# Two temporaries for a scan's output weights, idle matmuls in the start-up, and another rule for late fills, in a planned attention-and-scan kernel

## The chip, the cores and the metric

The kernel runs on one core of a Trainium2 chip. The metric is the device time of one execution in microseconds (us); the figure given for a kernel is the median of its runs. A profile is of one further execution.

## What is computed

Two independent things are computed and laid side by side. The left 640 columns of the output are a diagonal complex scan: `h[t] = Lam_bar * h[t-1] + B_bar x[t]` over 2048 steps with 640 states, then `y = 2 Re(C h) + x * Dskip`. The right 640 columns are attention with 32 query heads of width 20 that share one key and one value head.

```python
Lam_bar = exp(dt * Lam);  B_bar = ((Lam_bar - 1) / Lam)[:, None] * Bmat
h = Lam_bar * h + Bu[:, t, :]            # 2048 steps, complex, 640 states
y = 2.0 * einsum("blp,dp->bld", hseq, Cmat).real + x * Dskip

q = (x @ wq).reshape(B, S, 32, 20);  k = x @ wk;  v = x @ wv
p = softmax(einsum("bhqd,bkd->bhqk", q, k) * 20 ** -0.5)
out_b = einsum("bhqk,bkd->bhqd", p, v).reshape(B, S, 640) @ wo
```

In the kernel the factor `(Lam_bar - 1) / Lam` is not put into `B` but into `C`: the scan's output weights `CGre` and `CGim` are the complex product of `C` with that factor and 2. They are the weights of the first half of the title.

## The kernel before, in words

**Units of attention.** The scores are made in units of 128 keys by 512 queries of one head. 32 groups (8 for each block of 512 queries) hold 4 heads and 16 key chunks each, so 64 units: 2048 in all. A unit's exponential goes one of two ways. By ScalarE: a tile of 2 or 3 units is filled by TensorE in PSUM (`fill_op`, L1245; tiles `R0` of 3 banks and `R1` of 2), and one activation turns it into weights (`ex_op`, L1260; recorded at L1263). By VectorE ("D unit"): TensorE writes the scores into one of the banks `B0`, `B1` or the lent third bank of `R0`, one instruction turns them into the bits of a 16-bit float (`dx_op`, L1269), and three more shift copies of them (`sh_op`, L1274, up to three units in one instruction). The four copies are averaged by TensorE, which needs four PV matmuls for such a unit where the ScalarE way needs one. `want_d` (L1230) decides on each fill whether a D unit goes with it: when a bank is free and VectorE's backlog is small.

**The scan.** It runs in 20 units (4 blocks of 512 steps by 5 chunks of 128 states), through three threads. `scan_in` (L889): ten matmuls and two VectorE products (L901) of `B x` by rotations. `scan_unit` (L907): GpSimd adds in pieces of 128 columns (`uh`, 8 pieces), VectorE scans (L928, two instructions), GpSimd rotates back (`tm4` to `tm7`, 16 pieces) and combines into `W` (8 pieces); all GpSimd pieces are recorded at L917. `y_tile` (L943): the matmuls of `W` with `CGre` and `CGim`, with the output copy at L962. `W` of the next block is only written when the four y tiles of the block before are made. How far the scan may run ahead is set by `scan_open` (L1160), which spreads its 20 units over the first 0.6 or 0.7 of the attention units.

**The output weights.** For each of 5 chunks and each of `CGre`, `CGim`, GpSimd multiplies one raw half by a column of `sc` in five pieces of 128 columns (L858) into the one float32 temporary `ctmp`, which lies in `tm4` to `tm6`, and VectorE does the rest with one instruction over 640 columns (L860). The raw halves come by ten transposing DMAs on SyncE's queue (SP), into the memory of `W` (and `ostage` for the last chunk). In the thread `sc` all this stands behind the scan's constants, two memsets and the eight loads of `WO4`. `prog["c"]` turns 1 with the last of them, and the first rotation back waits for it.

**What sets the order.** Nothing is scheduled by hand. `Plan` (L21) keeps a clock for each engine and adds instructions one by one; `main` (L1127) collects the next instruction of every thread, of the fills, exponentials, shifts and PV matmuls, gives each a key (the planned begin, a bias by kind, a little noise) and takes the smallest. Engines' queues are then in exactly this order. The lengths are the planner's own: a GpSimd piece of 128 columns is planned at `max(0.2, 128/450 + 0.1)`, 0.38 us. A matmul other than a fill may go ahead of the next fill only if it ends before that fill's begin plus `after[n % 2]` (L1339), 0.1 to 0.2 us for even tiles and 0.35 to 0.5 us for odd ones. `vary` (L1113) draws biases and limits like these anew in each of 64 turns, from the list `SEEDS`. Where the planner sees TensorE wait long at low load it puts in matmuls by zero (`PV<-cs,VP`, L1418). At the start-up, `setup` ends with the thread `rest` (two VectorE copies of a half of K, the V matmuls, six more); until it is done no PV matmul is planned, while fills and exponentials already run.

Of the kernel before, what the change touches and what calls it, by code (L numbers as in the profile page):

```python
# [9 lines left out]
ALU = mybir.AluOpType  # L10
AX = mybir.AxisListType
FP32 = mybir.dt.float32
# [231 lines left out]
class _Kernel:  # L244
    S, D, H, DH = 2048, 640, 32, 20
    NC, NQB, NKC, NGG = 5, 4, 16, 8
# [8 lines left out]
    SPARE = 0.33  # L255
# [9 lines left out]
    SEEDS = (19006, 20002, 21006, 22006, 23001, 24003, 25001, 26002, 27008, 28003, 0, 30006, 31008, 32005, 33006,  # L265
# [28 lines left out]
    def alloc(self):  # L294
# [67 lines left out]
        self.ctmp = self.tm[:].rearrange("p i n -> p (i n)").bitcast(FP32)[:, 1024:1664]  # L362
# [454 lines left out]
    def scan_ops(self):  # L817
# [4 lines left out]
        sa, su, sr, sy, sc_ = [], [], [], [], []  # L822
        self.prog = prog = dict(x=0, a=0, u=0, s=0, r=0, y=0, w=0, c=0)
# [9 lines left out]
        ct = [f"tm{i}{h}" for i in (4, 5, 6) for h in self.PIECES]  # L833
# [14 lines left out]
        for c in range(NC):  # L848
            for i, nm in ((0, "cre"), (1, "cim")):
                sc_.append(self.dma(K.Craw[c][:, i, :], t[nm][:, 128 * c:128 * (c + 1)], f"craw{c}{i}",  # L850
                                    writes=[f"Craw{c}{i}"] + ([f"ostage{i}"] if c == 4 else []), tr=True, kb=160))
        for c in range(NC):
            cr, ci = K.Craw[c][:, 0, :], K.Craw[c][:, 1, :]
            keys = [f"Craw{c}0", f"Craw{c}1", "sc"] + (["ostage0", "ostage1"] if c == 4 else ws)
            for (dst, x, y, gx, gy, op, nm) in ((K.CGre, cr, ci, GRE, GIM, ALU.subtract, "CGre"),
                                                (K.CGim, ci, cr, NGRE, NGIM, ALU.add, "CGim")):
                for i in range(0, 640, 128):
                    pool(lambda e, y=y, c=c, gy=gy, i=i: e.tensor_scalar(K.ctmp[:, i:i + 128], y[:, i:i + 128], sc[:, gy, c:c + 1],  # L858
                                                                         None, op0=ALU.mult), keys, [f"ct{i}"] + ct * (i == 0), 128)
                dve(lambda e, dst=dst, x=x, op=op, c=c, gx=gx: e.scalar_tensor_tensor(  # L860
                    out=dst[:, c, :], in0=x, scalar=sc[:, gx, c:c + 1], in1=K.ctmp, op0=ALU.mult, op1=op),
                    keys + ct + [f"ct{i}" for i in range(0, 640, 128)], [nm], 695)
        sc_[-1].done = lambda: prog.update(c=1)
# [16 lines left out]
        sx = [o for b in (1, 2, 3) for o in self.load_xa(b, lambda b=b: prog["y"] >= 4 * (b - 1), lambda b=b: prog.update(x=b))]  # L880
        return sc_, sy, sr, su, sa, sx
# [25 lines left out]
    def scan_unit(self, dve, pool, back, b, c):  # L907
# [68 lines left out]
    def dense_ops(self, qb):  # L976
# [5 lines left out]
        have = lambda: all(g in self.normed for g in range(self.NGG * qb, self.NGG * qb + (6 if qb == self.NQB - 1 else 8))) and (  # L982
# [130 lines left out]
    def vary(self, seed):  # L1113
# [11 lines left out]
        self.open, self.first = r.choice((0.6, 0.7)), r.choice(("sy", "proj", None))  # L1125

    def main(self):  # L1127
# [24 lines left out]
        sc_, sy, sr, su, sa, sx = (deque(x) for x in self.scan_ops())  # L1152
# [16 lines left out]
        threads = [("rest", rest), ("norm", norm), ("dense", dense), ("proj", proj), ("qt", qt), ("qr", qr), ("sy", sy), ("sa", sa), ("su", su), ("sr", sr), ("sc", sc_), ("sx", sx), *fins]  # L1169
# [142 lines left out]
        while True:  # L1312
# [14 lines left out]
            if cur["fill"] < cur["act"] + 2 and any(x < 64 for x in taken) and not early:  # L1327
                n = cur["fill"]
                g = next(i for i in range(NG) if taken[i] < 64)
                if g in qt_done:  # L1330
# [8 lines left out]
                    t_fill = (t_fill, t_fill + self.after[n % 2])  # L1339
# [191 lines left out]
```

## Time and profile before

| | us |
|---|---|
| time, median of 3 runs (lowest, highest) | 770.16 (769.84, 772.17) |
| the profiled execution's own time | 770.28 |
| its span, first to last instruction | 768.6 |
| ScalarE busy, of it in the exponentials (L1263, 677 instructions) | 752.5, 733.1 |
| VectorE busy | 708.3 |
| TensorE busy | 704.8 |
| GpSimd busy, of it in the output weights (L858, 50 instructions) | 446.0, 41.8 |
| mean granted TensorE clock (1 is full) | 0.989 |

The profiled execution takes 1.7 us more than its span, and 0.1 us more than the median of the runs. In the group lines the columns are: line, engine, operation, output and input, count; then busy time in all and the mean of one in ns; then the idle time of the engine just before them and what ended it. In lines of stretches each engine's busy time stands with its instructions in brackets, then the clock granted to TensorE, the share of the DMA engines and GB/s. Exponentials overlap at their ends, so their mean of one is longer than their step.

### The profile page before, as it was taken

The numbers are of one execution on the slowest core, as the hardware profiler recorded it, in microseconds if no ns is written. First come the engines' busy times: TensorE is split into PE (matmuls) and PEld (weight loads), VectorE is DVE, ScalarE is ACT, GpSimd is POOL, SyncE is SP. The second block draws the span as 40 slices with busy tenths as digits, with TensorE's granted clock in tenths as the row PEclk, the third lists the DMA queues.
The fourth block names the chain that finished last, engine by engine and source line by source line (L and its number), as shares of the span: only waits on it lengthen the run. The fifth ranks groups of instructions, "written<-read, shape, count | busy, mean of one in ns | idle before, by whom it ended". The sixth has DMA issues, their size and how long they took to land.

```text
span 768.6 us, 16664 instructions
## 1 busy us (share of the span) xinstructions
PE 704.8 (92%) x6538; PEld 213.4 (28%) x6538; DVE 708.3 (92%) x1236; ACT 752.5 (98%) x710; POOL 446.0 (58%) x867
## 2 busy tenths in 40 slices
PE   5799988888889999998889999988889999889998
PEld 2222222222222333322223323322223332223333
DVE  5599999999998999999997999999999789999986
ACT  8999999999999999999999999999999999999995
POOL 5612354579989931088997300199986469990040
PEclk9899999899999999999999999999999999999999
DMA  9366301000021100220002100040000201000020
GB/s 186 57 143 134 74 16 49 8 24 14 3 51 30 42 8 27 56 60 15 15 9 67 42 23 9 23 93 10 15 15 28 66 33 34 14 15 17 18 61 35
DMA packets 61179, 31.50 MB, mean 41 GB/s; under 512 B 41510, under 2 KB 61102, under 8 KB 61102
## 3 DMA queue, kind: packets, MB, share of 16 engines
q1 hardware_dynamic: 59606, 30.14, 15.9%
q8 instruction: 52, 0.85, 0.5%
q10 hardware_dynamic: 1496, 0.30, 0.2%
q14 instruction: 25, 0.20, 0.1%
HBM read 9.21 MB, written 12.69 MB: 28 GB/s over the span
## 4 chain that ended last, share of the span: by engine, by line
ACT 74%; PE 15%; DVE 9%; POOL 1%; DMA 1%; issue 1%; ACTq 0%; DVEq 0%; POOLq 0%
ACT P L1263 72%; PE R L421 5%; PE PV L421 5%; PE B L421 4%; DVE Pd L1274 4%; DVE Pd L1269 3%; DVE hh L928 1%; DVE tm L901 1%; POOL tm L858 1%; DMA WO<-in_B_wk_dram 1%; ACT cs L691 1%; ACT Pd L690 0%; ACT KT L538 0%; DVE CGre L860 0%; ACT L503 0%
## 5 line engine op out<-in xcount | busy, mean ns | idle before, releaser
L1263 ACT ACTIVATE P<-R 128x1024 bf16<-128x1024 f32 (+1 forms) x677 | 733.1, 1354 | 4.3 <-PE R L421 1.8
L421 PE MATMUL R<-QT,KT 32*128 32x512 bf16 (+1 forms) x1685 | 266.9, 389 | 48.6 <-ACT P L1263 37.1
L1269 DVE TENSOR_SCALAR Pd<-B 128x512 int16<-128x512 f32 x363 | 245.5, 682 | 19.4 <-PE B L421 17.0
L1274 DVE TENSOR_SCALAR Pd<-Pd 128x1536 int16<-128x1536 int16 (+2 forms) x513 | 260.2, 541 | 0.4
L421 PE MATMUL PV<-Pd,VP 128*32 128x512 bf16 x1744 | 256.9, 386 | 2.0 <-DVE OTr L1307 1.0
L421 PE MATMUL PV<-P,VP 128*32 128x512 bf16 x1612 | 253.3, 389 | 0.7 <-DVE OTr L1307 0.6
L917 POOL TENSOR_TENSOR tm<-hh,cs 128x128 bf16<-128x128 f32 x320 | 163.9, 533 | 17.7 <-DVE hh L928 8.3
L421 PEld LDWEIGHTS R<-QT,KT 32*128 32x128 bf16 (+1 forms) x1685 | 66.1, 91 | 301.0 <-ACT P L1263 271.0
L421 PE MATMUL B<-QT,KT 32*128 32x512 bf16 x363 | 141.0, 389 | 0.0
L917 POOL TENSOR_TENSOR uh<-tm 128x128 bf16<-128x128 bf16 x160 | 81.0, 527 | 97.6 <-DVE tm L901 93.7
L917 POOL TENSOR_TENSOR W<-tm 128x128 bf16<-128x128 bf16 x160 | 93.5, 608 | 49.4 <-PE B L421 45.3
L421 PEld LDWEIGHTS PV<-Pd,VP 128*32 128x32 bf16 x1744 | 60.1, 94 | 65.7 <-issue 40.5
L421 PEld LDWEIGHTS PV<-P,VP 128*32 128x32 bf16 x1612 | 58.1, 94 | 58.8 <-issue 46.6
L1011 POOL TENSOR_TENSOR OTd<-OTd,rwide 128x128 bf16<-128x128 bf16 x80 | 33.2, 443 | 60.0 <-DMA OTd<-o_rows 58.2
L1269 DVE TENSOR_SCALAR Pd<-R 128x512 int16<-128x512 f32 x73 | 49.9, 683 | 3.0 <-PE R L421 2.4
L901 DVE TENSOR_TENSOR tm<-B,cs 128x1024 bf16<-128x1024 f32 x40 | 48.5, 1213 | 1.0 <-PE B L421 0.6
L858 POOL TENSOR_SCALAR tm<-W,sc 128x128 f32<-128x128 bf16 x40 | 32.3, 821 | 27.5 <-DVE CGre L860 15.9
L421 PE MATMUL B<-CGre,W 128*128 128x384 bf16 (+1 forms) x160 | 46.4, 305 | 0.0
L421 PE MATMUL B<-CGim,W 128*128 128x384 bf16 (+1 forms) x160 | 45.5, 299 | 0.0
L928 DVE TENSOR_TENSOR_SCAN hh<-sc,hini,uh 128x512 f32<-128x512 f32 x30 | 40.7, 1358 | 0.0
L421 PEld LDWEIGHTS B<-QT,KT 32*128 32x128 bf16 x363 | 32.9, 91 | 0.0
L421 PE MATMUL B<-xaT,BTre 128*128 128x512 bf16 x100 | 30.1, 384 | 0.1
(149 smaller groups left out, 437.2 us busy)
## 6 DMA issues: line engine op xcount, KB each, us to landing
o_rows<-OTr SPq DMA_DIRECT2D x32, 128.0 KB, 1.7
QT<-q_rows SPq DMA_DIRECT2D x30, 128.0 KB, 2.2
q_rows<-Qd SPq DMA_DIRECT2D x16, 160.0 KB, 2.9
OTd<-o_rows SPq DMA_DIRECT2D x16, 160.0 KB, 3.4
out_dram<-ystage SPq DMA_DIRECT2D x16, 160.0 KB, 1.9
out_dram<-ostage SPq DMA_DIRECT2D x12, 160.0 KB, 1.8
P<-in_B_wq_dram SPq DMA_DIRECT2D x1, 800.0 KB, 5.6
WO<-in_B_wo_dram SPq DMA_DIRECT2D x4, 200.0 KB, 3.4
```

The lines of the kernel that those rows point to most:

```text
L421: ins = e.matmul(o() if callable(o) else o, lhsT=l, rhs=r, start=st, stop=sp, skip_group_check=True, **kw)
L691: act(lambda e, c=c, b=b: e.activation(K.cs[:, c, :, :].rearrange("p i n -> p (i n)"), K.tri[:, 4 * b + 2:4 * b + 4, :].rearrange("p r n - ...
L858: pool(lambda e, y=y, c=c, gy=gy, i=i: e.tensor_scalar(K.ctmp[:, i:i + 128], y[:, i:i + 128], sc[:, gy, c:c + 1], None, op0=ALU.mult), key ...
L901: dve(lambda e, k=k, h=h: e.tensor_tensor(K.tm[:, 2 * k:2 * k + 2, :], bass.AP(tensor=K.BB, offset=512 * int(h.key[1]), ap=[[512 * self.BA ...
L917: put(lambda e, c0=c0, end=end: e.tensor_tensor(out[:, c0:end], a[:, c0:end], b[:, c0:end], op), reads, [writes + h], n, gate=None if i el ...
L928: dve(lambda e, ri=ri, ini=ini: e.tensor_tensor_scan(K.hh[:, ri, :], dec, K.uh[:, ri, :], ini, ALU.mult, ALU.add), ["sc", *(f"uh{ri}{h}" f ...
L1011: ops.append(Op("pool", lambda e, c=c, m=m: e.tensor_tensor(K.OTd[:, m, c], K.OTd[:, m, c], K.rwide[:, c], ALU.mult), rw + [f"OTe{dd}" for ...
L1263: return Op("act", lambda e: e.activation(dst, K.R[n % 2][:, 0:512 * size], ACT.Exp, scale=self.exp_scale), [f"R{n % 2}"] + ["R0c"] * (siz ...
L1269: return Op("dve", lambda e: e.tensor_scalar(K.Pd[:, 0, u, :], K.B[x][:, :], self.d_off, 0.0, op0=ALU.add, op1=ALU.max), [key], [f"Pd{u}_0 ...
L1274: return Op("dve", lambda e: e.tensor_scalar(K.Pd[:, i, a:b, :], K.Pd[:, 0, a:b, :], float(self.SHIFTS[i]), 0.0, op0=ALU.subtract, op1=ALU ...
```

## The change

Five edits and a new list of seeds.

1. **Output weights.** `ctmp` becomes two temporaries of 640 float32 columns in `OTd`, the attention's tile that is first written at the end of the first 8 groups. The thread `sc` is split in four: the raw loads (`sl`, now ahead of everything else of `sc`), the constants and `WO4` (`sc`), GpSimd's products (`sk`) and VectorE's halves (`sg`). The products may run one temporary ahead of VectorE.
2. **Planned length.** These 50 GpSimd pieces are planned at 0.58 us each.
3. **Gates.** The rotations back no longer wait for the weights; the writes of `W` do, and so do the first normalisation loads into `OTd` (`have`). The loads of `xa` for block 1 wait until VectorE has made three of the ten halves.
4. **Idle matmuls** (`WARM`). From the second copy of `rest` until the first PV matmul of group 0, where the planner sees TensorE wait over 0.25 us and its load in the last 3.4 us is under 0.8, it adds matmuls of the identity with `xbT` into `B0`.
5. **Late fills.** How late a fill may be goes by the size of the last tile that waits for ScalarE (3 units: 0.35 to 0.5 us; else 0.1 to 0.2 us), not by the parity of the tile's number. `open` may also be drawn as 0.8.

```diff
-    SPARE = 0.33
+    SPARE, WARM = 0.33, 0.8
-    SEEDS = (19006, 20002, 21006, 22006, 23001, 24003, 25001, 26002, 27008, 28003, 0, 30006, 31008, 32005, 33006,
+    SEEDS = (3005, 4007, 5003, 6007, 7004, 0, 9002, 10005, 11003, 12003, 13007, 14005, 0, 16003, 17005, 18006,
...
-        self.ctmp = self.tm[:].rearrange("p i n -> p (i n)").bitcast(FP32)[:, 1024:1664]
+        self.ctmp = self.OTd[:].rearrange("p c n -> p (c n)").bitcast(FP32).rearrange("p (i n) -> p i n", i=2)
...
+        for c in range(NC):
+            for i, nm in ((0, "cre"), (1, "cim")):
+                sl.append(self.dma(K.Craw[c][:, i, :], t[nm][:, 128 * c:128 * (c + 1)], f"craw{c}{i}",
+                                   writes=[f"Craw{c}{i}"] + ([f"ostage{i}"] if c == 4 else []), tr=True, kb=160,
+                                   done=(lambda c=c: prog.update(l=c + 1)) if i else None))
...
+        wide = lambda fn, reads, writes, n, **k: sk.append(Op("pool", fn, reads, writes, occ=0.58, **k))
...
+                for i in range(0, 640, 128):
+                    wide(lambda e, y=y, c=c, gy=gy, i=i, h=h: e.tensor_scalar(K.ctmp[:, h, i:i + 128], y[:, i:i + 128], sc[:, gy, c:c + 1],
+                                                                            None, op0=ALU.mult), keys, [f"ct{h}{i}"], 128,
+                         gate=lambda n=2 * c + h: prog["g"] >= n - 1 and prog["l"] > n // 2, done=(lambda n=2 * c + h + 1: prog.update(k=n)) if i == 512 else None)
+                cd(lambda e, dst=dst, x=x, op=op, c=c, gx=gx, h=h: e.scalar_tensor_tensor(
+                    out=dst[:, c, :], in0=x, scalar=sc[:, gx, c:c + 1], in1=K.ctmp[:, h, :], op0=ALU.mult, op1=op),
...
+                    gate=lambda n=2 * c + h: prog["k"] > n, done=lambda n=2 * c + h + 1: prog.update(g=n, c=int(n == 2 * NC)))
...
-        sx = [o for b in (1, 2, 3) for o in self.load_xa(b, lambda b=b: prog["y"] >= 4 * (b - 1), lambda b=b: prog.update(x=b))]
+        sx = [o for b in (1, 2, 3) for o in self.load_xa(b, lambda b=b: prog["y"] >= 4 * (b - 1) and prog["g"] > 2, lambda b=b: prog.update(x=b))]
...
-                   gate=lambda: prog["s"] > u and prog["c"], done=(lambda: prog.update(r=u + 1)) if i == 3 else None)
-        free = lambda: prog["y"] >= 4 * b
+                   gate=lambda: prog["s"] > u, done=(lambda: prog.update(r=u + 1)) if i == 3 else None)
+        free = lambda: prog["y"] >= 4 * b and prog["c"]
...
-        self.open, self.first = r.choice((0.6, 0.7)), r.choice(("sy", "proj", None))
+        self.open, self.first = r.choice((0.6, 0.7, 0.8)), r.choice(("sy", "proj", None))
...
+        self.still = False
+        rest[1].done = lambda: setattr(self, "still", True)
...
-                    t_fill = (t_fill, t_fill + self.after[n % 2])
+                    t_fill = (t_fill, t_fill + self.after[bool(tiles) and len(tiles[-1][1]) == 3])
...
+                if self.still and not any(begun[0]) and owner[0] in (None, "rest") and "B0" not in o.keys()[1]:
+                    while t - p.begin("pe", (), ("B0",)) > 0.25 and self.load(t) < self.WARM:
+                        self.go(self.mms([self.m1(K.B[0], K.ident[:, :], K.xbT[:, 0, 0:512], True, True)], ["ident", "xbT0"], ["B0"],
+                                         kind="zero"))
```

More of the change, by code (lines that the diff above doesn't have):

```diff
@@ L821, in scan_ops @@
         t = self.t
-        sa, su, sr, sy, sc_ = [], [], [], [], []
-        self.prog = prog = dict(x=0, a=0, u=0, s=0, r=0, y=0, w=0, c=0)
+        sa, su, sr, sy, sc_, sl = [], [], [], [], [], []
+        self.prog = prog = dict(x=0, a=0, u=0, s=0, r=0, y=0, w=0, c=0, k=0, g=0, l=0)
         def mk(ops, eng):
@@ L847, in scan_ops @@
                 sc_.append(self.dma(dst, src, f"wo{j}{w}", reads=["WO4"], writes=[f"WO4_{j}{w}"], kb=200 if w else 50))
[L848 to L863, printed above, removed]
         for b in range(4):
@@ L879, in scan_ops @@
                 self.y_tile(sy, mk(sy, "dve"), b, q)
-        sx = [o for b in (1, 2, 3) for o in self.load_xa(b, lambda b=b: prog["y"] >= 4 * (b - 1), lambda b=b: prog.update(x=b))]
-        return sc_, sy, sr, su, sa, sx
+        sx = [o for b in (1, 2, 3) for o in self.load_xa(b, lambda b=b: prog["y"] >= 4 * (b - 1) and prog["g"] > 2, lambda b=b: prog.update(x=b))]
+        return sl, sc_, sk, sg, sy, sr, su, sa, sx
     def load_xa(self, b, gate=None, done=None):
@@ L981, in dense_ops @@
         ops = []
-        have = lambda: all(g in self.normed for g in range(self.NGG * qb, self.NGG * qb + (6 if qb == self.NQB - 1 else 8))) and (
+        have = lambda: self.prog["c"] and all(g in self.normed for g in range(self.NGG * qb, self.NGG * qb + (6 if qb == self.NQB - 1 else 8))) and (
             qb == 0 or qb - 1 in self.projected)
@@ L1151, in main @@
         qr = deque(o for g in range(2, NG) for o in self.qr_ops(g, lambda g=g: qt_done.add(g)))
-        sc_, sy, sr, su, sa, sx = (deque(x) for x in self.scan_ops())
+        sl, sc_, sk, sg, sy, sr, su, sa, sx = (deque(x) for x in self.scan_ops())
         n_sa = len(sa)
```

12 lines of the change are left out of this document (10 added, 2 removed), and 8 rows, old and new, of the table SEEDS.

## The prediction

> **What bounds the kernel.** I read the engines' shares first, then the groups of instructions, the waits, and last the busy time by stretches, since a mean hides stages.
>
> ```profile
> PE 704.8 (92%) x6538; PEld 213.4 (28%) x6538; DVE 708.3 (92%) x1236; ACT 752.5 (98%) x710; POOL 446.0 (58%) x867
> ...
> L1263 ACT ACTIVATE P<-R 128x1024 bf16<-128x1024 f32 (+1 forms) x677 | 733.1, 1354 | 4.3 <-PE R L421 1.8
> ...
> L1269 DVE TENSOR_SCALAR Pd<-B 128x512 int16<-128x512 f32 x363 | 245.5, 682 | 19.4 <-PE B L421 17.0
> L1274 DVE TENSOR_SCALAR Pd<-Pd 128x1536 int16<-128x1536 int16 (+2 forms) x513 | 260.2, 541 | 0.4
> ...
> L1269 DVE TENSOR_SCALAR Pd<-R 128x512 int16<-128x512 f32 x73 | 49.9, 683 | 3.0 <-PE R L421 2.4
> ```
>
> ScalarE is the bound, but not a fixed one: it has what VectorE doesn't take. VectorE made 363 + 73 = 436 of the 2048 units, ScalarE the other 1612, at 733.1 / 1612 = 0.455 us each. A D unit costs VectorE 0.682 us and its share of the shifts, 260.2 / 436 = 0.597, together 1.28 us. So **1.28 us of VectorE time won anywhere is worth 0.455 us at the end**, a rate of 0.36, if TensorE can feed the unit. Before its exponentials ScalarE stands idle 4.3 us in all: little is to be had there directly.
>
> Where VectorE stands idle is seen in stretches (bounds at the stages of GpSimd's work):
>
> ```profile
> 62.00:162.00 100.00, 90.81 (x855) 23.89 (x855) 97.73 (x176) 98.88 (x93) 47.55 (x67) 0.95 0.21 46
> 162.00:262.00 100.00, 90.84 (x824) 25.03 (x820) 95.10 (x148) 100.00 (x94) 91.59 (x181) 1.00 0.10 28
> ...
> 402.00:430.00 28.00, 27.60 (x242) 9.45 (x239) 22.52 (x38) 27.93 (x26) 22.75 (x49) 1.00 0.19 52
> 430.00:500.00 70.00, 69.72 (x660) 21.39 (x656) 66.15 (x123) 69.83 (x68) 4.43 (x12) 1.00 0.08 24
> ...
> 590.00:620.00 30.00, 29.69 (x295) 11.16 (x294) 24.25 (x48) 30.00 (x28) 8.15 (x21) 1.00 0.19 54
> ...
> 695.00:750.00 55.00, 52.37 (x551) 18.63 (x550) 49.28 (x100) 55.00 (x51) 8.10 (x20) 1.00 0.12 34
> ```
>
> The columns are TensorE, its weight loads, VectorE, ScalarE, GpSimd. VectorE is idle 2.3 us in the first 100, but 5.5, 3.9, 5.8 and 5.7 us in the last four stretches; all ten stretches that I cut between 62 and 750 us hold 37.1 us. TensorE is nearly full there (27.6 of 28, 29.7 of 30), as y tiles, projection and scan meet, and has 18 us free in the first two. The load is badly spread.
>
> **Why: the output weights.** They run from 75.8 to 162.7 us, and these waits carry it (engine and line, whom it waited for, us in total, times, longest):
>
> ```profile
> POOL uh L917 <- DVE tm L901: 93.7, 6, 47.6
> ...
> POOL tm L858 <- DVE CGre L860: 20.3, 5, 8.4
> ...
> POOL tm L858 <- DVE CGim L860: 16.0, 4, 5.7
> ...
> DVE CGre L860 <- POOL tm L858: 0.5, 1, 0.5
> ```
>
> GpSimd multiplies for about 4 us (41.8 us in 50 pieces), then waits for VectorE, whose half stands deep in its own queue: 36.3 us in all. VectorE waits 0.5 us. Meanwhile no rotation back may start, and by 200 us four of the 20 scan units have their products, where the opening rule (48 + 59 units of attention for each scan unit at 0.6, at some 2.8 a us) would have let seven begin.
>
> **The clock.** Per us, with the clock in the third column from the end:
>
> ```profile
> 26.00:27.00 1.00, 0.39 (x3) 0.10 (x3) 0.86 (x3) 1.00 (x3) 0.97 (x2) 1.00 0.01 2
> 27.00:28.00 1.00, 0.39 (x2) 0.10 (x2) 1.00 (x4) 1.00 (x1) 0.69 (x2) 1.00 0.07 13
> 28.00:29.00 1.00, 0.62 (x4) 0.18 (x4) 0.16 (x1) 1.00 (x2) 0.73 (x3) 0.61 0.01 3
> 29.00:30.00 1.00, 1.00 (x3) 0.13 (x3) 0.00 (x0) 1.00 (x2) 0.71 (x4) 0.50 0.00 0
> ...
> 34.00:35.00 1.00, 1.00 (x10) 0.11 (x2) 0.72 (x3) 0.55 (x1) 0.19 (x1) 0.50 0.06 0
> ```
>
> It is 0.50 from about 28.4 to 35 us, after 3 us in which TensorE was 0 to 0.4 busy; again at 120.7 to 123.6 and 141 to 147.6 us. ScalarE loses 0.62 us to the first spell (before 34.45) and 1.1 us to the third (0.46 and 0.60 are its longest gaps).
>
> **The change, part by part.** All sums are against the profiled execution, 770.28 us (span 768.6 and 1.7 around it), which lies 0.1 above the median.
>
> *Idle matmuls.* TensorE waits 1.23, 0.52 and 0.95 us for ScalarE between 25 and 28.4 us. The nearest row for one is the start-up's own `R<-xbT,WO`: four in 1.03 us, 0.26 each; so ten at most fit, in time in which TensorE has nothing else. Best end: ScalarE's 0.62 us, and VectorE's idle time before 33.34, 35.63 and 33.95 us (5.17 + 0.91 + 0.62 = 6.7 us, times 0.36 = 2.4 us): 3.0 won. Worst: each of ten holds a fill back 0.26 us and ScalarE has no cover: 2.6 lost. The cover is the other PSUM tile, 1.08 us (733.1 / 677) against a cold fill of 0.61. Most of VectorE's 5.17 us stays, as D units begin only after 24 units of group 0, and fills go at ScalarE's pace. I take **0.8 won**.
>
> By the Trainium skill, "TensorE: Matmul & The Clock Gate", section "Why this matters for your kernels", only gaps of more than about 3 us between matmuls bring the half clock back; by that there was nothing to keep warm here. The trace disagrees: its longest gap ahead of the first spell is 1.23 us.
>
> *The weights moved.* What moves: 50 pieces on GpSimd (41.8 us), ten VectorE halves (0.875 each, the same number as before), and on SP ten transposes at 1.27 us of queue time each, 12.7 in all. Those went out at 69.7 to 85.6; now they go out when the transposes of `BTim` end, near 52.5, ahead of the eight loads of `WO4` (not needed before the first projection, after 200 us) and of the five `xaT` transposes of block 1 (59.1 to 67.4; next used near 234). GpSimd is idle from 42 to 64.9, so the products can begin near 58. With one temporary in hand its work until the last product is 41.8 + 3.5 + 8.1 + 3.4 (two `uh` and one rotation beside it) = 57 us: the weights are there near **115 to 120 us rather than 162**. The group 2 queries (`QT<-q_rows` at 65.3 us) also pass SP; a transpose ahead of them costs 1.3 us, and only what exceeds the 3 us or so by which that load runs ahead of its use would reach ScalarE.
>
> What this gives is not GpSimd's 36 us, which lie on nobody's path, but a scan some 45 us earlier. First, TensorE gets scan matmuls at 110 to 160 us, where it is 0.77 to 0.91 busy and goes cold: the 1.1 us of ScalarE there, best end 1.8 with VectorE's 1.8 us idle between 136 and 146 times 0.36, worst 0 (the spell comes elsewhere): **1.1 won**. Second, the y tiles leave the full stretches. Of the 37.1 us idle no more than 13.2 us (times 0.36) can be had; half would be 6.6; a quarter, 9.3 us or 7 D units, is **3.3 won**. At the other end the redraw by new seeds gives nothing or takes some back: the D rate of the stretches runs from 12 in 28 us (0.43) to 67 in 100 (0.67), and ten units are 4.6 us. I take the quarter, since of the last four stretches' 20.9 us about half is lost where y tiles and projection meet.
>
> *Late fills.* 80 or so of the even tiles have two units, and the rule was generous to the fill behind them. The 4.3 us of ScalarE's idle time before exponentials less 1.7 counted above leave 2.6; ends 1.0 won, 1.0 lost (other matmuls pushed back): **0.3 won**. `open` at 0.8 is part of the redraw.
>
> Sum: 0.8 + 1.1 + 3.3 + 0.3 = 5.5; 770.28 - 5.5 = 764.8, and **764.7** beside the median. Next in line, if ScalarE has fewer units, is TensorE: a D unit adds three PV matmuls there, four of which run side by side in about 0.22 us, so 7 units cost it 1.2 us of 64 idle.
>
> **Rivals.**
>
> *Idle time moves, nothing more.* The weights come early, but the scan's pace is set by its chain over blocks (GpSimd waits 45.3 us for y tiles: `POOL W <- PE B`), and the D count stays within two of 436. Then only the start-up's 0.8 is left: 769.4. For it: three long GpSimd waits that one temporary doesn't cause. Against: those waits begin later because the weights did.
>
> *VectorE waits for GpSimd (slower).* Before, VectorE almost never waited for products, since its half was planned late. The new plan lets it follow a product after 5 x 0.58 = 2.9 us and what the plan adds for VectorE's own traffic. In the trace five pieces take 3.05 to 5.32 us, 4.18 in the mean, one alone 0.60 to 2.63. If the planner puts each half right behind its product, VectorE stands 1.28 us at the head of its queue ten times, 12.8 us, 10 D units, 4.6 us at the end: 770.2 + 4.6 - 0.8 = **774.0**. It decides where the planned distance falls below 1.3 us; the D units and shifts behind wait with it, and so do the B banks. For it: the spread of the piece. Against: the planner counts port time too, and 0.58 is near the median of 0.605.
>
> The Trainium skill, "GPSIMD Engine Reference", section "Key points", says that GpSimd shares its SBUF interfaces with VectorE and contends with instructions that use two ports or two SBUF inputs. The trace agrees (0.60 to 2.63 us for one piece), which speaks for this rival.
>
> *The clock gains nothing.* If only long gaps cool TensorE, as the first page has it, the two clock terms (1.9) go: 766.6.
>
> **Chances.** Forecast 0.52, clock gains nothing 0.11, idle time moves 0.15, VectorE waits or a poor draw of seeds 0.22. A difference of 0.3% (2.3 us) is about what a measurement can tell here: faster means below 767.9, slower above 772.5. So faster 0.63, same 0.15, slower 0.22. The range runs from half of the idle time won with the best start-up (770.2 - 6.6 - 3.0 - 1.4, about 759) to the slower rival with a little more (775).
>
> **What would show it.** Right: `CGim` finished near 120 us; clock 1.00 from 25 to 150 us; 440 to 446 D units and 667 to 673 exponentials; less VectorE idle time after 400 us. Wrong: a wait of VectorE's L860 for L858 of more than 3 us; a D count at or under 436; y tiles that meet the projection elsewhere, so that stretches with a full TensorE and an idle VectorE are as long as before; a gap of ScalarE at 65 to 75 us (queries behind the transposes).

## The result, and the profile after

The changed kernel takes **776.36 us** (median of 5 runs, 774.10 to 777.62) beside 769.84 for the kernel before in the same series; the ratio is 1.0086 with an interval of 1.0065 to 1.0108. It is slower by 0.9%, on the other side of the forecast and 1.4 us beyond the upper end of the range. The profiled execution took 777.62 us, the longest of the five; its span is 775.9, 7.3 more than before.

The engines and the groups that carried the prediction, from the page of the kernel after:

```profile
PE 703.9 (91%) x6501; PEld 213.2 (27%) x6501; DVE 707.2 (91%) x1227; ACT 756.6 (98%) x707; POOL 443.9 (57%) x867
...
L1270 ACT ACTIVATE P<-R 128x1024 bf16<-128x1024 f32 (+1 forms) x674 | 737.2, 1361 | 8.0 <-PE R L421 4.0
...
L1276 DVE TENSOR_SCALAR Pd<-B 128x512 int16<-128x512 f32 x367 | 248.5, 683 | 24.3 <-PE B L421 21.5
L1281 DVE TENSOR_SCALAR Pd<-Pd 128x1536 int16<-128x1536 int16 (+2 forms) x513 | 261.8, 545 | 1.0
...
L1276 DVE TENSOR_SCALAR Pd<-R 128x512 int16<-128x512 f32 x60 | 40.9, 682 | 3.2 <-PE R L421 2.8
```

Read the counts first: 367 + 60 = 427 D units, not 436 and not the forecast's 443. Nine units went back to ScalarE: its exponentials are busy 4.1 us longer (737.2 against 733.1; 9 x 0.455 = 4.1). Then the column ahead of the arrow: ScalarE stood idle 8.0 us before exponentials, 3.7 more than before. 4.1 + 3.7 = 7.8 is the whole loss of 7.3 and a little over. VectorE is busy as long as before with less to show for it: by forms, the shifts of the kernel before and then of the kernel after are

```profile
L1274 DVE TENSOR_SCALAR Pd<-Pd 128x1536 int16<-128x1536 int16 x354 | 205.5, 608 | 0.2
...
L1274 DVE TENSOR_SCALAR Pd<-Pd 128x1024 int16<-128x1024 int16 x87 | 35.8, 450 | 0.2
...
L1274 DVE TENSOR_SCALAR Pd<-Pd 128x512 int16<-128x512 int16 x72 | 20.9, 323 | 0.1
```

```profile
L1281 DVE TENSOR_SCALAR Pd<-Pd 128x1536 int16<-128x1536 int16 x336 | 199.4, 618 | 0.6
...
L1281 DVE TENSOR_SCALAR Pd<-Pd 128x1024 int16<-128x1024 int16 x96 | 42.4, 474 | 0.3
...
L1281 DVE TENSOR_SCALAR Pd<-Pd 128x512 int16<-128x512 int16 x81 | 22.8, 325 | 0.1
```

The same 513 instructions shift nine units fewer: 0.613 us a unit instead of 0.597, 7 us of VectorE in all. Roughly half of that is that more of them hold one or two units, the other half that each takes longer (618 ns instead of 608 for three units, 474 instead of 450 for two).

Did the idle time of VectorE come back? The stretches that the prediction used, and 620 to 695 beside them (TensorE, weight loads, VectorE, ScalarE, GpSimd, clock):

```profile
62.00:162.00 100.00, 87.94 (x768) 22.69 (x766) 95.17 (x146) 96.74 (x90) 88.21 (x144) 0.95 0.22 48
162.00:262.00 100.00, 92.58 (x850) 27.50 (x849) 95.13 (x156) 99.81 (x91) 68.48 (x138) 1.00 0.09 25
...
402.00:430.00 28.00, 27.70 (x258) 8.25 (x250) 26.73 (x47) 28.00 (x28) 13.30 (x29) 1.00 0.33 68
430.00:500.00 70.00, 64.01 (x590) 18.82 (x592) 67.12 (x107) 69.86 (x64) 61.86 (x127) 1.00 0.09 27
...
590.00:620.00 30.00, 24.74 (x235) 6.72 (x235) 29.39 (x44) 29.88 (x28) 27.99 (x52) 1.00 0.17 43
620.00:695.00 75.00, 72.15 (x715) 24.25 (x713) 66.44 (x136) 75.00 (x70) 15.03 (x31) 1.00 0.09 31
695.00:750.00 55.00, 44.64 (x470) 11.85 (x469) 49.33 (x95) 54.98 (x51) 7.01 (x17) 0.97 0.08 21
```

In the kernel before, the one of these that the prediction doesn't show was

```profile
620.00:695.00 75.00, 69.10 (x633) 19.78 (x630) 73.13 (x121) 74.61 (x69) 68.30 (x128) 1.00 0.08 24
```

402 to 430 and 590 to 620 are mended: VectorE is idle 1.3 and 0.6 us there, where it was 5.5 and 5.8. But 620 to 695 now loses 8.6 us (1.9 before) and the first stretch 4.8 (2.3). Over 62 to 750 us it is 39.0 us against 37.1. The idle time moved.

The D units moved with it. These are their first instructions alone (VectorE busy, count), in the kernel before and then in the kernel after:

```profile
62.00:162.00 100.00, 44.60 (x67) 0.95 0.21 46
402.00:430.00 28.00, 8.19 (x12) 1.00 0.19 52
```

```profile
62.00:162.00 100.00, 37.13 (x55) 0.95 0.22 48
402.00:430.00 28.00, 13.47 (x20) 1.00 0.33 68
```

402 to 430 gains eight and 590 to 620 four (15 to 19), but the first stretch loses twelve. VectorE's work for the scan (its products and its scans), which now comes earlier, takes 17.1 us there instead of 8.5, and VectorE was 97.7% busy there before.

Where the loss arises in time is seen at the ends of the groups (the copy `OTr<-PV`). The kernel after ends group 0 at 54.3 us, 1.8 later than before, group 3 at 127.4 (+7.8) and group 5 at 175.7 (+10.3); group 24 is 10.5 late, the last 7.3. So the kernel after is 10 us late by 176 us and wins some of it back at the end. Not all of the 10.3 us is the chip's doing: the planner itself has group 5 end 5.0 us later (165.0 against 160.0 us by its own clock) and its last instruction 1.7 later; the other 5.3 are the chip behind the plan. Before exponentials ScalarE was idle 3.6 us in 20 to 56 us (1.5 before), 3.0 in 56 to 130 (none before) and 0.4 in 130 to 176 (1.1 before).

**The wait at 118 us.** VectorE's queue, and then GpSimd's, in the kernel after (start, duration; idle time before it in brackets):

```profile
116.25 0.62 DVE L1281 TENSOR_SCALAR Pd<-Pd 128x1536 int16<-128x1536 int16 x1
118.81 0.89 DVE L854 SCALAR_TENSOR_TENSOR CGre<-ostage,sc,OTd 128x640 bf16<-128x640 bf16 x1 [1.94 <-POOL OTd L851]
119.62 1.95 DVE L1281 TENSOR_SCALAR Pd<-Pd 128x1536 int16<-128x1536 int16 x3
```

```profile
113.81 3.20 POOL L851 TENSOR_SCALAR OTd<-ostage,sc 128x128 f32<-128x128 bf16 x3
116.98 0.42 POOL L922 TENSOR_TENSOR uh<-tm 128x128 bf16<-128x128 bf16 x1
117.49 1.76 POOL L851 TENSOR_SCALAR OTd<-ostage,sc 128x128 f32<-128x128 bf16 x3
```

Three products took 3.20 us, where the planner counts 1.74. VectorE reached its half 1.94 us too soon; three shifts stood behind it, and TensorE's PV matmuls behind those. TensorE had little to do in that time, and the clock answered (same columns as the stretches):

```profile
119.00:120.00 1.00, 0.23 (x4) 0.00 (x0) 1.00 (x2) 1.00 (x2) 0.92 (x3) 1.00 0.06 16
120.00:121.00 1.00, 0.55 (x7) 0.20 (x7) 1.00 (x2) 0.62 (x1) 1.00 (x2) 1.00 0.00 0
...
122.00:123.00 1.00, 0.71 (x12) 0.28 (x12) 1.00 (x3) 0.27 (x2) 0.96 (x2) 0.50 0.00 0
123.00:124.00 1.00, 1.00 (x10) 0.15 (x6) 1.00 (x3) 1.00 (x1) 0.92 (x3) 0.50 0.00 0
```

The clock is 0.50 from 121.9 to 128.7 us; the longest gaps of ScalarE from 120 to 130 us are 0.60, 0.73, 0.62 and 0.81 us. They are nearly all of its 3.0 us of idle time between 56 and 130 us. How much of that the wait makes, the experiments must show.

**The start.** The idle matmuls ran (the trace has seven of them, from 23.7 to 29.9 us, and the plan has seven; the expectations below say eight), and TensorE was full, at half clock:

```profile
27.00:28.00 1.00, 1.00 (x5) 0.21 (x4) 0.00 (x0) 0.54 (x2) 0.71 (x3) 0.50 0.00 0
28.00:29.00 1.00, 1.00 (x4) 0.21 (x3) 0.00 (x0) 1.00 (x1) 0.71 (x4) 0.50 0.04 8
29.00:30.00 1.00, 0.94 (x5) 0.21 (x4) 0.00 (x0) 1.00 (x2) 0.68 (x5) 0.50 0.04 0
30.00:31.00 1.00, 1.00 (x5) 0.13 (x2) 0.00 (x0) 0.54 (x2) 0.71 (x4) 0.50 0.05 0
```

The spell lasts from 22.9 to 33.2 us, longer than before (28.2 to 35.0), and began ahead of the first idle matmul. Each of them takes 0.59 to 0.61 us, 0.54 of it before the next matmul can begin; the prediction's sum had 0.26.

**GpSimd.** Its waits for VectorE's halves (36.3 us) are gone and those for VectorE's products fell from 93.7 us to 27.1, but it now waits 84.1 us for y tiles, 45.3 before (waits: total, times, longest):

```profile
POOL W L922 <- PE B L421: 84.1, 3, 36.0
POOL uh L922 <- DVE tm L906: 27.1, 6, 12.2
...
DVE CGre L854 <- POOL OTd L851: 1.9, 1, 1.9
```

The products ran from 59.8 to 127.2 us, but VectorE's last half stood in its queue until 133.8.

### The profile page after: what moved, and what is told of

Same layout as the page of the kernel before. It is cut to its first block, busy times and chain, and to the rows that moved or that the text cites. A ratio compares the mean times of both kernels' runs of the same rounds, so it can differ in the third digit from the quotient of the medians.

```text
span 775.9 us, 16579 instructions
## 1 busy us (share of the span) xinstructions
PE 703.9 (91%) x6501; PEld 213.2 (27%) x6501; DVE 707.2 (91%) x1227; ACT 756.6 (98%) x707; POOL 443.9 (57%) x867
## 4 chain that ended last, share of the span: by engine, by line
ACT 80%; PE 9%; DVE 7%; POOL 2%; issue 1%; DMA 1%; ACTq 0%; POOLq 0%; DVEq 0%
ACT P L1270 78%; PE R L421 3%; PE B L421 3%; PE PV L421 3%; DVE Pd L1281 3%; DVE Pd L1276 2%; POOL OTd L851 2%; DVE tm L906 1%; POOL uh L922 1%; ACT cs L691 1%; DMA WO<-in_B_wk_dram 1%; DVE hh L933 0%; ACT Pd L690 0%; ACT KT L538 0%; DVE CGim L854 0%
## 5 line engine op out<-in xcount | busy, mean ns | idle before, releaser
L1270 ACT ACTIVATE P<-R 128x1024 bf16<-128x1024 f32 (+1 forms) x674 | 737.2, 1361 | 8.0 <-PE R L421 4.0
L1276 DVE TENSOR_SCALAR Pd<-B 128x512 int16<-128x512 f32 x367 | 248.5, 683 | 24.3 <-PE B L421 21.5
L421 PE MATMUL PV<-P,VP 128*32 128x512 bf16 x1621 | 257.3, 388 | 2.3 <-DVE Pd L1281 1.5
L922 POOL TENSOR_TENSOR tm<-hh,cs 128x128 bf16<-128x128 f32 x320 | 167.1, 544 | 21.2 <-DVE hh L933 13.4
L922 POOL TENSOR_TENSOR W<-tm 128x128 bf16<-128x128 bf16 x160 | 86.1, 559 | 88.6 <-PE B L421 84.1
L1016 POOL TENSOR_TENSOR OTd<-OTd,rwide 128x128 bf16<-128x128 bf16 x80 | 37.2, 491 | 112.5 <-DMA OTd<-o_rows 110.7
L922 POOL TENSOR_TENSOR uh<-tm 128x128 bf16<-128x128 bf16 x160 | 83.5, 540 | 31.2 <-DVE tm L906 27.1
L1276 DVE TENSOR_SCALAR Pd<-R 128x512 int16<-128x512 f32 x60 | 40.9, 682 | 3.2 <-PE R L421 2.8
L851 POOL TENSOR_SCALAR OTd<-W,sc 128x128 f32<-128x128 bf16 x40 | 30.3, 769 | 16.5 <-DMA W<-in_A_C_im_dram 15.1
```

What stands on the lines that cost most here:

```text
L421: ins = e.matmul(o() if callable(o) else o, lhsT=l, rhs=r, start=st, stop=sp, skip_group_check=True, **kw)
L851: wide(lambda e, y=y, c=c, gy=gy, i=i, h=h: e.tensor_scalar(K.ctmp[:, h, i:i + 128], y[:, i:i + 128], sc[:, gy, c:c + 1], None, op0=ALU.mu ...
L922: put(lambda e, c0=c0, end=end: e.tensor_tensor(out[:, c0:end], a[:, c0:end], b[:, c0:end], op), reads, [writes + h], n, gate=None if i el ...
L1016: ops.append(Op("pool", lambda e, c=c, m=m: e.tensor_tensor(K.OTd[:, m, c], K.OTd[:, m, c], K.rwide[:, c], ALU.mult), rw + [f"OTe{dd}" for ...
L1270: return Op("act", lambda e: e.activation(dst, K.R[n % 2][:, 0:512 * size], ACT.Exp, scale=self.exp_scale), [f"R{n % 2}"] + ["R0c"] * (siz ...
L1276: return Op("dve", lambda e: e.tensor_scalar(K.Pd[:, 0, u, :], K.B[x][:, :], self.d_off, 0.0, op0=ALU.add, op1=ALU.max), [key], [f"Pd{u}_0 ...
```

## The experiments

Two theories at first. **A:** the loss is made by the two added things, idle matmuls and early products, and goes with them. **B:** it is the order that the new list of seeds draws, and would be there without them. **C** is B carried to the kernel before: another list alone costs as much.

**idle_short.** The changed kernel, its order kept; the idle matmuls write 8 columns (the edits here and below are shown in short).

```diff
-    e.matmul(B0, lhsT=ident, rhs=xbT[:, 0, 0:512])
+    e.matmul(B0[:, 0:8], lhsT=ident, rhs=xbT[:, 0, 0:8])
```

> The changed kernel, every instruction in the same order and planned the same, but the eight idle matmuls of the start-up have 8 columns on the chip instead of 512. Theory A (the idle matmuls stand in front of fills on a TensorE at half clock; that is what the start-up lost): ScalarE's idle time before exponentials between 24 and 37 us falls from 3.5 us to 1.5 or less, group 0 ends at 52.5 to 53 us instead of 54.3, and the time falls by 1 to 2 us, to 774.5 to 775.5. Rival B (the half clock itself, which began at 22.9 us before the first idle matmul, is what cost the time, and the idle matmuls at least end it): the half clock lasts as long or longer, the time stays within 0.7 us of 776.4 or rises.

Measured: 776.51 us (774.55 to 777.03), ratio 1.0078 (1.0056 to 1.0100). Group 0 ends 0.5 us sooner, and nothing of that can be told at the end. ScalarE's idle time between 24 and 37 us falls from 3.6 us to 2.8, not to 1.5, and the half clock is there all the same, 10.2 us of it. Theory A misses; the time is the rival's.

**prod_short** and **both_short.** The order kept; each GpSimd product covers 16 columns and VectorE's half reads these 16 forty times, so that the output weights are not those of the kernel. both_short has the short idle matmuls too.

```diff
-    e.tensor_scalar(K.ctmp[:, h, i:i + 128], y[:, i:i + 128], ...)
+    e.tensor_scalar(K.ctmp[:, h, i:i + 16], y[:, i:i + 16], ...)
```

> The changed kernel in the same order, but each of GpSimd's 50 product pieces makes 16 columns instead of 128, and VectorE's halves read the first 16 over and over: the output weights are left wrong, VectorE's work is the same. Theory A (VectorE's one wait of 1.9 us at 118.8 us for a product started the half-clock spell at 121.9 us, which cost ScalarE 2.8 us): wait and spell go, group 3 ends near 123 to 124 us instead of 127.4, the time falls by 2.5 to 4 us, to 772.5 to 774. Rival B (TensorE is lightly used there anyway, so the spell comes a few us later, as it came twice in the kernel before): the wait goes, but the spell stays and the time falls by less than 1.5 us.

> Both shortenings at once, same order (output weights left wrong). If both theories A hold, the time falls by 3.5 to 6 us, to 770.5 to 773, and what is left above the 769.8 of the kernel before, 1 to 3 us, is the order itself: the planner's own clock ends 1.8 us later, with 9 D units fewer. If both rivals hold, 775 or more, and the order is worth 5 us and more.

Measured: 774.32 us (ratio 1.0054, 1.0032 to 1.0076) and 772.78 us (1.0040, 1.0027 to 1.0053). The first is 0.3 us above theory A's range, the second within it. In both the wait at 118 us is gone, and with it the spell at 121.9 us (the next is at 148, 3.41 us long): both_short, per us,

```profile
119.00:120.00 1.00, 0.64 (x12) 0.22 (x12) 1.00 (x3) 1.00 (x2) 0.91 (x3) 1.00 0.00 0
120.00:121.00 1.00, 1.00 (x14) 0.20 (x6) 1.00 (x3) 1.00 (x2) 1.00 (x3) 1.00 0.00 0
...
122.00:123.00 1.00, 0.81 (x12) 0.21 (x8) 1.00 (x3) 1.00 (x2) 0.96 (x2) 1.00 0.03 8
```

In both_short ScalarE's idle time before exponentials is 4.2 us, as in the kernel before (4.3). So A holds for 3.6 of some 7 us: that much goes when GpSimd's products and the idle matmuls cost next to nothing. 3.7 stay, with the nine D units fewer: B for that half.

**before_redraw** and **before_redraw_b.** The kernel before, with nothing changed but `SEEDS`: lists from a quick search on the planner alone (nine candidates a turn, the best planned end kept). The planned end is the planner's own clock after the last store on SyncE's queue: 753.4 us for the kernel before, 755.1 for the kernel after.

> The kernel before with another list of seeds and nothing else changed; the planner's own clock ends at 763.2 instead of 753.4 us. Theory C (the order that the seeds draw decides the time, and the chip follows the planner at a nearly fixed distance, 15 us in the kernel before): 763.2 + 15.2 + 1.7, so 778 to 782, slower than either kernel, with no edit made. Rival (the chip evens such differences out, since ScalarE is never idle): within 3 us of 769.8.

> The kernel before with a third list of seeds (same search, base number 3), planned end 763.9 us. By a lag of 15 to 16 us as in its other two lists: 779 to 780. If the lag of one code differs from draw to draw by as much as the kernel after differs from the kernel before (5.6 us), it may come out anywhere from 778 to 785.

Measured: 778.61 us (ratio 1.0112) and 779.58 (1.0131). C holds: another list alone costs 9 to 11 us, more than the whole change. This is the price of a quick search in place of the one behind the kernel's own list, which plans 9.8 to 10.5 us shorter; the two quick lists lie 1.0 us apart. And the time follows the plan: 15.7, 15.4 and 15.6 us above the planned end in three draws. (The kernel before itself had medians of 768.46 to 770.27 us in the series of these experiments, so its 15.7 could be 15.1 to 16.9.)

**after_redraw_a** and **after_redraw_b.** The changed kernel with two more lists from the same search.

> The changed kernel with another list of seeds, found by a search of the same kind and size as that of before_redraw (nine candidates a turn, the best planned end kept; same base number). Its planned end is 760.0 us by the same clock that gives 753.4 for the kernel before, 755.1 for the kernel after and 763.2 for before_redraw, which ran 15.7, 21.3 and 15.4 us above their planned ends. Theory: the time is the planned end plus a lag, and the lag of the kernel after is larger by the wait and clock spell at 119 to 129 us that its draw happened to have (prod_short and both_short gave 2.1 and 3.6 us of it back): another draw of the changed code then lags like the others, 15 to 18 us, and gives 775 to 778. Rival: the larger lag belongs to the changed code (products on GpSimd longer than planned, idle matmuls), whatever the draw: then 21 us above the plan, 780 to 782. If the edits by themselves help at equal search, it is below the 778.6 of before_redraw; if they hurt, above.

> As after_redraw_a with a third list (base number 3, as the kernel after's own list has it), planned end 760.4 us. Theory that the lag belongs to the one draw: 775.5 to 778.5. Rival that it belongs to the changed code: 780.5 to 782.5. The two lists of one code also show how far two draws of equal planned end differ on the chip.

Measured: 782.36 us (ratio 1.0164, 1.0140 to 1.0188) and 780.32 (1.0128, 1.0093 to 1.0163), 22.3 and 19.9 us above the plan. The theory that the lag was one draw's bad luck falls, and the rival holds: the changed code lags its plan by 20 to 22 us in all three draws. The edits make plans that are 3.1 and 3.5 us shorter at equal search, and times that are 3.7 and 0.7 us longer; the second pair, run in one series, can't be told apart (777.83 to 781.24 and 778.79 to 781.19). They don't bring D units either: 423 and 428, where the two lists of the kernel before have 429 and 431. VectorE waits for a product 3.6 us in all in the one and 1.7 in the other. Such waits alone don't make the lag: before_redraw has 2.1 us of them and lags 15.4.

**after_whole** and **before_whole.** A real cure, the order kept: of each five products the first four are left out and the fifth does all 640 columns; in after_whole the idle matmuls go too.

```diff
-    for i in range(0, 640, 128): tensor_scalar(ctmp[:, h, i:i + 128], ...)
+    tensor_scalar(ctmp[:, h, :], ...)          # at the place of the fifth
```

> The changed kernel in its own planned order, every other instruction kept: each group of five GpSimd products of 128 columns becomes one instruction of 640 columns at the place of the fifth (the outputs are the same), and the eight idle matmuls are left out. Theory: GpSimd's products are later than planned (0.79 us each in the mean against 0.58), VectorE waits for them, and with the idle matmuls they make the 5.6 us by which this code lags its plan more than the kernel before. In prod_short a product of 16 columns still took 0.48 us, so most of a piece is a fixed cost, and one instruction of 640 columns should take some 1.4 to 2.2 us in place of 3.95: the time falls as in both_short, to 772 to 773.5. Rival: GpSimd's cost is columns shared with VectorE, not instructions: the long one takes 3 us or more, VectorE waits as before, and only the start is won: 775 to 776.5.

> The kernel before in its own planned order, with the same edit alone: one product of 640 columns at the place of the fifth of each five. It tells what the products themselves cost where VectorE's half stands late in its queue and waits for them only 0.5 us in all. Theory: nothing waits for them, so little is won: 768 to 769.3 beside 769.1. Rival: the products slow the shifts beside them (1536 columns 550 ns alone, 643 with GpSimd at work), so that 20 us less of GpSimd work gives VectorE back 2 to 3 us and the end about 1 us: 767.5 to 768.

Measured: 776.54 us (1.0078, 1.0061 to 1.0095) and 769.27 (0.9985, 0.9971 to 0.9999, beside 770.27). For before_whole the theory's figure came. For after_whole the time is about the rival's, but neither mechanism is what happened: the products took 1.88 to 3.01 us, 2.13 in the mean (the theory had 1.4 to 2.2), and no half of VectorE waited, yet nothing was won. There is no half clock between 33 and 613 us in it either, and still ScalarE is idle 1.5 us between 56 and 130 us, half of the kernel after's 3.0: the wait and the spell account for the other half at most. Against both_short, instruction by instruction in the same order, VectorE loses 2.3 us by the end of group 3, in longer instructions and not in waits, and 1.4 more at a half-clock spell at 613.5 us. What grew is seen between 56 and 128 us, in both_short and then in after_whole:

```profile
L1283 DVE TENSOR_SCALAR Pd<-Pd 128x1536 int16<-128x1536 int16 x40 | 24.2, 618 | 0.0
...
L935 DVE TENSOR_TENSOR_SCAN hh<-sc,uh 128x512 f32<-128x512 f32 x4 | 4.9, 1214 | 0.0
```

```profile
L1301 DVE TENSOR_SCALAR Pd<-Pd 128x1536 int16<-128x1536 int16 x37 | 24.0, 660 | 0.0
...
L953 DVE TENSOR_TENSOR_SCAN hh<-sc,uh 128x512 f32<-128x512 f32 x4 | 5.4, 1346 | 0.0
```

So the price of a product to VectorE is its columns as well as its end. before_whole is 1.0 us faster than the kernel before in the same series; that is less than the 2.3 us that the prediction took for telling it from no change.

**cure_redraw, cure_redraw_b, long_redraw.** The changed code with products planned at 0.80 us (they measure 0.79 in the mean); the first two also without idle matmuls. New lists each.

```diff
-    SPARE, WARM = 0.33, 0.8
+    SPARE, WARM = 0.33, 0.0                    # not in long_redraw
-    wide = lambda ...: sk.append(Op("pool", fn, reads, writes, occ=0.58, **k))
+    wide = lambda ...: sk.append(Op("pool", fn, reads, writes, occ=0.80, **k))
```

> The changed code with the products planned at 0.80 us each instead of 0.58 and without idle matmuls, and a list of seeds from a search of the same size and base number as after_redraw_b. Its planned end is 764.3 us. Theory: what the changed code lagged more than the kernel before (lags 21.3, 22.4 and 19.9 against 15.7, 15.4 and 15.7) was the planned length of the products and the idle matmuls. Then the lag is 15 to 17.5, the time 779.5 to 782, and at the ends of groups 0 and 5 the lag is near 2 to 3 and 4 to 6 us (the changed kernel's: 4.7 and 10.7). Rival: the lag comes from something else in the changed code (rotations back ahead of the weights, the gates, the rule for late fills): 20 to 22 us, 784 to 786.

> As cure_redraw (products planned at 0.80 us, no idle matmuls) with a second list of seeds (same search, base number 19); planned end 764.9 us. In cure_redraw the early part went as the theory has it (lag 3.0 us at the end of group 0, 5.8 at the end of group 5), but the lag at the end was 20.0 by the median, where the theory had 15 to 17.5: 2 to 3 us more than in the kernel before came after group 20 and in the last 10 us. Theory, as it now stands: the products and idle matmuls make the early part of the lag, and what cure_redraw lost late belongs to that draw: 16 to 18.5 us here, 781 to 783.5. Rival: another part of the changed code (rotations back ahead of the weights, gates, late fills) makes a late lag whatever the draw: 19.5 to 21, 784.5 to 786.

> The changed code with the products planned at 0.80 us, the idle matmuls kept, and a list of seeds from a search some three times as large; planned end 760.1 us. Theory: the idle matmuls cost 0.5 to 1.5 us at the start and the longer planned products take away the jump between groups 1 and 5 (lag at group 0 near 4.5, at group 5 near 7, where the three lists with 0.58 had 10.0 to 10.7); in all 17.5 to 19.5 us of lag, 777.5 to 779.5. Rival, that the late fills or gates make the lag: 780.5 to 782.

Measured: 784.22, 781.55 and 781.77 us (ratios 1.0186, 1.0170, 1.0164). The lag behind the plan, in us, at the ends of three groups in the profiled execution, and of the median time behind the planned end (for the kernel before 769.07, the median of 17 runs beside the first experiments):

| kernel | planned end | group 0 | group 5 | group 31 | time |
|---|---|---|---|---|---|
| before | 753.4 | 2.9 | 5.4 | 13.6 | 15.7 |
| before_redraw | 763.2 | 2.1 | 3.7 | 11.6 | 15.4 |
| before_redraw_b | 763.9 | 1.8 | 5.3 | 12.8 | 15.6 |
| after | 755.1 | 4.7 | 10.7 | 19.1 | 21.2 |
| after_redraw_a | 760.0 | 4.6 | 10.1 | 19.0 | 22.3 |
| after_redraw_b | 760.4 | 5.1 | 10.0 | 17.3 | 19.9 |
| both_short | 755.1 | 3.5 | 6.2 | 14.3 | 17.6 |
| after_whole | 755.1 | 3.7 | 8.4 | 18.1 | 21.4 |
| long_redraw | 760.1 | 5.1 | 9.1 | 19.2 | 21.7 |
| cure_redraw | 764.3 | 3.0 | 5.8 | 15.4 | 20.0 |
| cure_redraw_b | 764.9 | 2.7 | 4.8 | 13.6 | 16.7 |

In long_redraw and cure_redraw_b the planner's ScalarE queue ends after SyncE's, at 760.9 and 765.5 us; by that their last column is 20.9 and 16.1.

**Group 0** separates the draws cleanly: 4.6 to 5.1 us of lag where the code adds idle matmuls to the plan and the chip runs them, 1.8 to 3.0 where it plans none. Taking them off the chip alone gives back 0.5 to 1.2 us (4.2 in idle_short, 3.5 in both_short, 3.7 in after_whole); the rest stays with the plan. A likely reason is the planned clock, for the planner reckons it from the load that it plans, and idle matmuls count: between 18 and 60 us it has TensorE slow for some 7 us in the kernel before and for under 1 us in the kernel after, in whose trace it is slow for 10.2. That this clock is the reason is argued, not shown. before_whole, in the order of the kernel before, was slow for 13.65 us at its start (21.8 to 35.4) and ended group 0 at 52.5 us all the same, as the kernel before did with 6.8.

**Between group 0 and group 5** the lag grows by 6.0 us in the kernel after and by 4.9 in idle_short, but by 2.5 in prod_short and 2.7 in both_short, where the three draws of the kernel before have 2.5, 1.6 and 3.5. So in this order the excess of the jump is the work of GpSimd's products, and after_whole, with their columns in fewer instructions, keeps part of it (4.7). With their true length planned and no idle matmuls (the two cure draws) it is 2.8 and 2.1. long_redraw, with the true length but with idle matmuls, missed the theory's 777.5 to 779.5: its lag grows by 4.0 to 9.1. Why the longer planned products didn't take the jump away there is open; its half-clock spells at 61.6, 109.4 and 146.9 us lie in that stretch.

cure_redraw's time still came out at the rival's figure; cure_redraw_b, the second draw, has 16.7 and the late lag of the kernel before, so as far as one draw can tell the late part was that of the first. No run takes the gates or the rule for late fills out alone.

And the gain of the edits is gone with the cure: planned ends of 764.3 and 764.9, beside 763.2 and 763.9 for the kernel before at equal search. As far as two lists each can tell, the shorter plans were made of products that the chip takes longer for and of a clock that it did not give. The D units say the same: 425 and 426, and 422 in long_redraw.

## Why the prediction was wrong, step by step

- **A quarter of the idle time, 7 D units, 3.3 won: this step failed.** 427 units instead of 443 make 4.1 us lost. The scan did move as forecast: its first `W` is written at 127 us instead of 171, its last y tile copied at 683 instead of 742, and late stretches got their D units. But the sum put at nothing what the moved work displaces where it lands: between 62 and 162 us, where VectorE was full, its scan work doubled (8.5 to 17.1 us) and twelve D units went. That is how the stretches read; no run moves the scan alone. From 62 to 750 us VectorE's idle time stayed about what it was (39.0 us against 37.1), and its shifts cost 7 us more. I took a share of an idle time as if the new plan started from the old one; it is a new draw of the whole order, which mended 402 to 430 and 590 to 620 us and broke 620 to 695. The loss of D units is not one list's bad luck: the six lists of the changed code make 422 to 428, the three of the code before 429, 431 and 436. Which of the edits does it, no run separates.
- **The same loss by the plan: 1.7 us planned, 5.5 us lag.** The kernel after is planned 1.7 us longer (755.1 against 753.4) and lags its plan by 21.2 us instead of 15.7. The planned part is the list: at equal search the edits plan 3.1 to 3.5 us shorter, but the kernel before's own list beats its quick lists by some 10 us and the kernel after's by some 5. I had bounded the redraw by ten units, 4.6 us, and put it into a rival. The sum has no term for the lag; 3.6 us of it went in both_short.
- **Idle matmuls, 0.8 won: wrong sign.** ScalarE is idle 2.1 us more in 20 to 56 us. idle_short gives 0.5 us back at group 0, both_short 1.1. The rest need be no effect of the matmuls on the chip: before_redraw, without them, also shows the half clock for 10.2 us (21.6 to 31.8) and ScalarE idle 3.6 us before these exponentials. The spell of 6.8 us that I started from is the shortest of all the start-ups here; the others have 10.24 or 13.65 us, before_whole too, whose start is planned like that of the kernel before. And an idle matmul holds TensorE for 0.54 us at half clock, not for 0.26.
- **Weights at 115 to 120 us rather than 162: half right.** The products began at 59.8 us (58 was forecast) and ended at 127.2; the last half of VectorE began at 133.8, for it waits in VectorE's queue like any other. GpSimd's waits for VectorE's halves did go, and its waits for the y tiles grew from 45.3 to 84.1 us, the pace that the first rival named.
- **The clock spells at 110 to 160 us gone, 1.1 won: wrong.** There are as many us of half clock in that stretch as before, 10.24: 121.9 to 128.7 and 152.6 to 156.1. The first goes when L854 doesn't wait for L851 (prod_short, both_short, after_whole). ScalarE was idle 2.3 us more between 56 and 176.
- **Late fills, 0.3 won: not separated.** After 176 us ScalarE's idle time before exponentials is about 1.0 us against 1.6, so no more than 0.6 was won there.
- **The conversion held on ScalarE's side:** 0.455 us for a D unit gives 4.1 us for nine, as measured. On VectorE's side it didn't: nine units are 11.5 us at 1.28 each, and VectorE's idle time grew by 1.9; dearer shifts took 7.
- **Rivals.** VectorE did wait for GpSimd, though not ten times 1.28 us: once 1.94, below the 3 us that I had named as the sign. 774.0 was the nearest figure, by another path: nine D units were lost, but not to such waits. The rule of the Trainium skill that the third rival drew on ("TensorE: Matmul & The Clock Gate", section "Why this matters for your kernels": only gaps over some 3 us cool TensorE) would not have the spell at 121.9 either: TensorE's longest gap in the ten us before it is 1.22 us, at 119.2.

## What to carry to other kernels

Where a planner with drawn parameters sets the order, price the redraw first, by drawing again without the edit and with the same search: here it moved the time by 9 to 11 us, more than any term of the sum. Then compare the plan with the trace at checkpoints: a constant lag (15.4 to 15.7 us in three draws) says that a planned gain can be trusted, and a lag that grows with the edit says that the chip doesn't do what the planner was told, here of the products' length and probably of the clock. A consumer planned right behind a producer of uncertain length can cost more than the wait, when short work for TensorE and the clock come on top; it need not (2.1 us of such waits in before_redraw, and no more lag).

## What the runs showed of the hardware

- **The half clock comes in steps of 3.41 us and goes with use, not with gaps.** Spells last 3.41, 6.83, 10.24 or 13.65 us, and within a run all begin a whole number of such steps apart. The Trainium skill, "TensorE: Matmul & The Clock Gate", section "What's actually happening", has a free-running window of 3413 ns, and the traces agree. Cut into these windows, the 14 traces show between 60 and 765 us: every full-clock window with TensorE less than 0.575 busy was followed by the half clock (ten of them), none with more than 0.69, and of those between some (26). The Trainium skill also says there that one busy window brings the full clock back; in the kernel after TensorE was 0.94 to 1.00 busy in every us from 26 to 33, through two windows, before the clock rose at 33.2.
- **Much of the spread between runs of one kernel goes with that clock:** the kernel before ran 768.2 us with a mean clock of 0.991 and 772.4 with 0.982.
- **A product on GpSimd has a fixed cost and a cost by column.** 16 columns took 0.32 us with no shift beside them, 128 columns 0.60, 640 columns 1.88: some 0.28 us and 2.5 ns a column. In the mean, with VectorE at work, they took 0.48, 0.79 and 2.1. The fixed part is a little over half of a piece of 128 columns and a small part of one of 640, so the expectation of after_whole, that most of a piece is fixed cost, had its size too high.
- **Contention is partial.** A shift of 1536 columns takes 0.55 us alone, up to 0.84 beside GpSimd's adds, up to 1.08 beside a product of 640 columns. The Trainium skill, "SBUF — State Buffer", section "SBUF: two separate sides", has a lock that is held for the whole instruction. In after_whole a shift that began 0.13 us into a product of 1.89 us, at 73.1 us, took 1.07 us and ended 0.7 us ahead of the product; by such a lock it would have taken over 2 us.
